# k and q as 32 by 32 squares: VectorE's block transpose in place of TensorE's turning, in an mLSTM cell with a SwiGLU block behind it

## The chip, the cores and the metric

The kernel runs on one core of one Trainium2 chip. The metric is the device time of a run in microseconds (us). The kernel before took 577.31 us (median of 3 runs, 577.21 to 579.02).

## What is computed

Two blocks follow each other. The first is an mLSTM cell over 4 batches of 8 heads, 768 tokens, head size 40, all float32. The second is a SwiGLU feed-forward block on its output, with model size 320 and inner size 1536. Cut to what matters:

```python
for t in range(S):
    m_new = np.maximum(f_gate[:, :, t] + m, i_gate[:, :, t])
    f_stab = np.exp(f_gate[:, :, t] + m - m_new)
    i_stab = np.exp(i_gate[:, :, t] - m_new)
    C = f_stab * C + i_stab * einsum('bhd,bhe->bhde', vt, kt)
    n = f_stab * n + i_stab * kt
    h_tilde = einsum('bhde,bhe->bhd', C, qt)
    denom = np.maximum(np.abs(einsum('bhd,bhd->bh', n, qt)), 1.0)
    y[:, :, t] = sigmoid(o_gate[:, :, t]) * h_tilde / denom
x = y.transpose(0, 2, 1, 3).reshape(B * S, H * D)
g = x @ w_gate
out = (g * sigmoid(g) * (x @ w_val)) @ w_out
```

The weights arrive as float64 and are narrowed to float32 in the kernel.

## The kernel before

The 768 tokens are cut into 6 groups of 128 (`NG`), each of two halves of 64. The cell works on a group at a time in the parallel form: scores of q against k, weights from the gates, a value product, and a running state C. The feed-forward block works on the same groups, 512 columns wide (4 batches of 128 tokens). While the feed-forward of group g runs, the cell of group n = g + 1 is computed between its pieces, and the inputs of group f = g + 2 are loaded. Nothing is scheduled by a planner: the order on every engine is the order in which the code issues (`manual_schedule`), and the pieces are put by hand into lists called `slots`, one list for each of 12 hidden chunks.

**The feed-forward.** `hidden` (L594) makes one chunk: 20 matmuls into two PSUM buffers of the tag "gen" (L599), of which there are four, then a silu on ScalarE (L604) and a product on VectorE (L605) that empty the two. Chunk m + 2 thus needs the buffers of chunk m. After 12 chunks, `project` (L612, matmuls L615) forms the output of each of the 4 batches; `result` (L607) copies it on ScalarE (L609, two buffers) and stores it from SyncE (L610). For group 0 `project_all` (L618, matmuls L622) does the four batches together, with a dictionary `after` (L689) of cell work between its 12 steps.

**Where k and q go.** `load` (L112) brings k and q with tokens on partitions: 128 partitions by 16 heads by 40 numbers, two such transfers to a tensor and group, issued on SyncE (L113). The scores (L305, matmuls L309) need them with the head dimension on partitions, in `kT` and `qT`: 128 partitions (two heads of 64, of which 40 are filled) by 16 head pairs by 128 tokens. `turn` (L299) makes these: for each half of the heads, `turn_one` (L289) runs 16 transposes for k and 16 for q on TensorE against an identity (L294, tile `tp_kq`), into PSUM buffers of the tag "cell", and copies them out, one copy on ScalarE and one on VectorE each (L117, L119). `add` (L325, matmuls L330), the state's increment, takes k as loaded, with tokens on partitions. `attend` (L344) reads qT again.

**The order around it.** Group 0 and group 1 have their own code; group 1's turning stands in slots 6 and 7 of the first hidden phase (L676, L677). For group 2, the loads of v, k, q and o_gate are issued during `project_all(0)` (L691, L693), behind the weights' load (`weights_load`, L400). After `project_all(0)` come the exponentials of the weights and the sigmoids of o_gate on ScalarE (L701 to L704) and the value products on GpSimd (`weigh_values`, L705, L706). Then the memory of the first phase is released and the pool `late` takes it (L707, L708). In the loop over g from 1 (L712), slots 0 and 1 hold `turn` for the two halves of the heads of group n (L716, L717), slot 3 the scores (L718), slot 5 the state's increment (L720), slots 7 and 9 `attend`; the loads of group f stand in slots 1 (q), 5 (k), 9 (v and weights) and 10 (o_gate) (L728 to L731).

Of the kernel before, what the change touches and what calls it, by code (L numbers as in the profile page):

```python
# [9 lines left out]
F32 = mybir.dt.float32  # L10
# [8 lines left out]
L = 128  # L19
# [5 lines left out]
def kernel(  # L25
# [18 lines left out]
    nc = tc.nc  # L44
    B, H, S, D = q.shape
# [4 lines left out]
    PP = BH // 2  # L50
# [8 lines left out]
    UA = UH // 2  # L59
# [16 lines left out]
    def bank(name, tag="cell"):  # L76
        return psum.tile([128, 512], F32, name=name, tag=tag)

    def half(i):
        return slice(i * SUB, (i + 1) * SUB)  # L80
# [4 lines left out]
    k_sb = const.tile([128, BH, DP], F32)  # L85
    q_sb = const.tile([128, BH, DP], F32)
    v_sb = const.tile([128, BH, D1], F32)
    o_sb = const.tile([128, BH, D], F32)
    w_sb = const.tile([128, BH, SUB], F32)
    vw_sb = const.tile([128, BH, D1], F32)  # L90
    kT = const.tile([128, PP, L], F32)
    qT = const.tile([128, PP, L], F32)
# [22 lines left out]
    def copy(eng, dst, src):  # L115
        if eng is nc.scalar:
            nc.scalar.copy(dst, src)  # L117
        else:
            eng.tensor_copy(dst, src)  # L119
# [125 lines left out]
    for u in range(B):  # L245
        r = slice(u * BH, (u + 1) * BH)
# [42 lines left out]
    def turn_one(P, src, dst, engs):  # L289
        tp = [bank("tp_kq").rearrange("p (a t) -> p a t", t=SUB) for _ in range(2)]  # L290
        for a in range(UA):
            h = P * UH + 2 * a
            for i in range(2):
                nc.tensor.transpose(tp[i][:, a, :], src[half(i), h:h + 2, :].rearrange("p h d -> p (h d)"),  # L294
                                    ident[half(i), half(i)])
        for i in range(2):
            copy(engs[i], dst[:, P * UA:(P + 1) * UA, half(i)], tp[i])

    def turn(P, eng_k, eng_q):  # L299
        turn_one(P, k_sb, kT, eng_k)  # L300
        turn_one(P, q_sb, qT, eng_q)

    QUAD = ((0, 0), (1, 1), (0, 1), (1, 0))

# [13 lines left out]
    def weigh_values(eng, P):  # L318
        eng.tensor_tensor(vw_sb[:, heads(P)], v_sb[:, heads(P)], w_sb[:, heads(P), last].to_broadcast([128, UH, D1]),  # L319
                          op=ALU.mult)  # L320
# [84 lines left out]
    def weights_sub(n, P):  # L405
        gb = g_T[:, n, heads(P)].unsqueeze(2).to_broadcast([128, UH, SUB])
        nc.vector.tensor_tensor(w_sb[:, heads(P)], gb, w_sb[:, heads(P)], op=ALU.subtract)  # L407

    def weights_mask(P):
        for i in range(2):  # L410
            w = w_sb[half(i), heads(P)]
            nc.gpsimd.affine_select(w, w, compare_op=ALU.is_ge, fill=NEG, base=0, pattern=[[0, UH], [1, SUB]],  # L412
                                    channel_multiplier=-1)

    def weights_exp(P):
        nc.scalar.activation(w_sb[:, heads(P)], w_sb[:, heads(P)], AF.Exp)

    def sig(P):
        nc.scalar.activation(o_sb[:, heads(P)], o_sb[:, heads(P)], AF.Sigmoid)
# [10 lines left out]
    A, V, G = nc.scalar, nc.vector, nc.gpsimd  # L430
# [163 lines left out]
    def hidden(g, m, first=()):  # L594
        ps = [bank("gv_ps", "gen") for _ in range(2)]
        x = xT(g)
        for kc in range(NKC):
            for i in range(2):
                nc.tensor.matmul(ps[i], lhsT=wgv_sb[half(i), m, PAIRS[kc][i], :], rhs=x[half(i), kc, :],  # L599
                                 start=(kc == 0), stop=(kc == NKC - 1))  # L600
        for f in first:
            f()
        sg = work.tile([128, TW], F32, name="sg")
        nc.scalar.activation(sg, ps[0], AF.Silu)  # L604
        nc.vector.tensor_tensor(hid(g, m), sg, ps[1], op=ALU.mult)  # L605
# [6 lines left out]
    def project(g, u):  # L612
        p = bank("o_ps", "gen")[:, 0:DM]
        for m in range(NFC):
            nc.tensor.matmul(p, lhsT=hid(g, m)[:, ts(u, L)], rhs=wo_sb[:, m, :], start=(m == 0), stop=(m == NFC - 1))  # L615
        result(g, u, p)
# [43 lines left out]
    def load_all(dst, a, n):  # L660
        for P in range(2):
            load(dst, a, n, P)

    run = lambda f, *a: (lambda: f(*a))
# [6 lines left out]
    slots = {  # L671
        0: [run(first_state, 1, A), run(load_all, k_sb, k, 1), run(load_all, q_sb, q, 1), run(late_maxima)],
        1: [run(decay_rows), run(piece_load, 6, h_sb[:, NH - NKC:])],
        2: [run(late_turns), run(weights_load, 1)],
        3: [run(decay), run(load_all, v_sb, v, 1)],
        6: [run(turn, 0, (A, A), (A, V)), run(piece_load, 7)],  # L676
        7: [run(turn, 1, (A, A), (A, V)), run(weights_sub, 1, 0), run(weights_sub, 1, 1), run(weights_mask, 0),  # L677
            run(weights_mask, 1)],
        8: [run(weights_exp, 0), run(weights_exp, 1), run(weigh_values, G, 0), run(weigh_values, G, 1),
# [5 lines left out]
    for m in range(NFC):  # L685
# [2 lines left out]
            f()  # L688
    after = {  # L689
        0: [run(do_attend, 1, 1), run(convert, 14), run(sig, 0), run(sig, 1), run(do_gate, 0)],  # L690
        1: [run(do_gather, 1, 1), run(weights_load, 2), run(load_all, v_sb, v, 2)],  # L691
        2: [run(do_divide, 0), run(convert, 15)],
        3: [run(do_divide, 1), run(load_all, k_sb, k, 2), run(load_all, q_sb, q, 2), run(load_all, o_sb, o_gate, 2)],  # L693
        4: [run(convert, 16), run(seam, 1, 0, (A, V, A, V))],
        5: [run(seam, 1, 1, (A, V, A, V))],
        6: [run(convert, 17)],
# [11 lines left out]
    late = ctx.enter_context(tc.tile_pool(name="late", bufs=1))  # L708
    xTs.append(late.tile([128, NKC, TW], F32, name="xT1"))


    for g in range(1, NG):  # L712
        n, f = g + 1, g + 2
        slots = {m: [] for m in range(NFC)}
        if n < NG:
            slots[0] = [run(turn, 0, (A, V), (A, V))]  # L716
            slots[1] = [run(turn, 1, (A, V), (A, V))]  # L717
            slots[3] = [run(do_scores), run(do_weigh, 0)]  # L718
            slots[4] = [run(do_weigh, 1)]
            slots[5] = [run(do_add), run(do_state, 2 * n, 0)]  # L720
            slots[6] = [run(do_state, 2 * n, 1)]
            slots[7] = [run(do_attend, n, 0), run(do_gather, n, 0)]
            slots[8] = [run(do_divide, 0)]
            slots[9] = [run(do_attend, n, 1), run(do_gather, n, 1)]
            slots[10] = [run(do_divide, 1), run(seam, n, 0, (A, V, A, V))]
            slots[11] = [run(seam, n, 1, (A, V, A, V))]
        if f < NG:
            slots[1].append(run(load_all, q_sb, q, f))  # L728
            slots[5].append(run(load_all, k_sb, k, f))
            slots[9] += [run(load_all, v_sb, v, f), run(weights_load, f)]  # L730
            slots[10].append(run(load_all, o_sb, o_gate, f))  # L731
        for m in range(NFC):
            hidden(g, m)
            for s in slots[m]:
                s()
        for u in range(B):
            if f < NG and u < 2:
                weights_sub(f, u)
                weights_mask(u)
            if f < NG and u == 2:  # L740
                weights_exp(0)
                weights_exp(1)
                sig(0)
                sig(1)
                weigh_values(nc.gpsimd, 0)
                weigh_values(nc.gpsimd, 1)
            project(g, u)
# [30 lines left out]
```

## Time and profile before

| What | Value |
|---|---|
| median of 3 runs | 577.31 us |
| profiled execution | 579.26 us, of which the span of the profile 577.5 us |
| TensorE matmul busy | 567.9 us (98% of the span) |
| VectorE busy | 211.7 us (37%) |
| ScalarE busy | 151.0 us (26%) |
| GpSimd busy | 102.4 us (18%) |
| SyncE's and ScalarE's transfer queue | 127284 packets, 32.92 MB, 33.0% of 16 engines' span |
| turning, `tp_kq` L294, matmuls | 160 for k and 160 for q, 222 ns each, overlapping |
| copies out of `tp_kq` | 584 to 592 ns on ScalarE, 680 to 684 ns on VectorE |
| a k or q load, two transfers of 320 KB | 6.4 us (k) and 4.0 us (q) from issue to landing, median |

How to read the profile: the span is one execution on the chip, in us. PE is TensorE's matmul, DVE VectorE, ACT ScalarE, POOL GpSimd, and SPq SyncE's queue; L294 is line 294 of the kernel. A group of instructions is given as line, engine, operation, output and input, shape and count. The chain of waits is the work that ended last, followed back from the last instruction: at each step to what released it, or to the instruction before it on its engine. In the chain in order of time, the columns are start, length, what, and how many instructions were merged. In the table of stretches, each line is a stretch of time with its length, then busy time and number of instructions of PE, PE's weight loads, DVE, ACT and POOL, then the granted TensorE clock, the mean busy share of the DMA engines (over 1 where packets overlap), and the rate in GB/s. The time of a transfer's row on SyncE is that of issuing it, not of the movement.

### The profile page before, as it was taken

To read this page: it belongs to the slowest core of one execution; us is meant where nothing else is said; L and a number is where in the kernel's file an instruction comes from. 1 tells how busy PE (TensorE), PEld (TensorE's weight loads), DVE (VectorE), ACT (ScalarE), POOL (GpSimd) and SP (SyncE) were. 2 spreads that over 40 slices of the span, in tenths; PEclk is the share of its full clock that TensorE was granted. 3 is DMA by queue.
4 is the path that set the end of the run, shared out by engine and by line. 5 is a ranking of instruction groups with operands and counts; after the bars stand their busy time and mean duration, and the time that the engine had idled before them with its cause. 6 is when DMAs were issued, how large, how long until landed. Compare 5 with 4: busy or idle time off the path is not lost.

```text
span 577.5 us, 12169 instructions
## 1 busy us (share of the span) xinstructions
PE 567.9 (98%) x5407; PEld 332.0 (57%) x5407; DVE 211.7 (37%) x378; ACT 151.0 (26%) x237; POOL 102.4 (18%) x101
## 2 busy tenths in 40 slices
PE   9998998999999999999999999999999999999997
PEld 4955454765655676455576555567555567544475
DVE  5776595860325600234620224630223630011100
ACT  3366554427210223201115210114311010011100
POOL 2132345463001141001132001232001110000000
PEclk9999998999999999999999999999999999999999
DMA  9999992494141800313620304450000000000000
GB/s 126 182 283 175 177 252 93 86 148 93 25 48 24 144 23 24 47 24 48 112 43 33 48 1 56 78 92 23 12 2 2 3 1 24 23 1 0 1 23 23
DMA packets 129915, 37.85 MB, mean 66 GB/s; under 512 B 120424, under 2 KB 125032, under 8 KB 129864
## 3 DMA queue, kind: packets, MB, share of 16 engines
q1 hardware_dynamic: 127284, 32.92, 33.0%
q10 hardware_dynamic: 2580, 4.16, 3.3%
q8 instruction: 42, 0.69, 0.5%
q14 instruction: 9, 0.07, 0.0%
HBM read 33.06 MB, written 4.01 MB: 64 GB/s over the span
## 4 chain that ended last, share of the span: by engine, by line
PE 91%; DMA 3%; ACT 3%; DVE 1%; issue 1%; POOL 0%; ACTq 0%; DVEq 0%; POOLq 0%
PE gv_ps L599 49%; PE o_ps L615 23%; PE o_ps L622 4%; DMA raw<-in_moe_w_val_dram 3%; PE inter L349 2%; PE intra L354 2%; PE add L330 2%; PE tp_kq L294 1%; PE sp L309 1%; PE first_y L486 1%; PE tp_x L395 1%; PE burn L425 1%; PE tp_x L517 1%; PE tp_kq L465 1%; PE sp L475 1%
## 5 line engine op out<-in xcount | busy, mean ns | idle before, releaser
L599 PE MATMUL gv_ps<-xT,wgv_sb 64*128 64x512 f32 x1440 | 322.2, 596 | 1.8 <-POOL wgv_sb L204 1.8
L599 PEld LDWEIGHTS gv_ps<-xT,wgv_sb 64*128 64x128 f32 x1440 | 139.6, 188 | 154.9 <-issue 150.2
L605 DVE TENSOR_TENSOR h_sb<-sg,gv_ps 128x512 f32<-128x512 f32 x72 | 49.5, 687 | 302.5 <-ACT sg L604 287.3
L615 PE MATMUL o_ps<-wo_sb,h_sb 128*128 128x320 f32 x480 | 130.5, 433 | 0.0
L615 PEld LDWEIGHTS o_ps<-wo_sb,h_sb 128*128 128x128 f32 x480 | 90.8, 190 | 38.2 <-issue 0.8
L604 ACT ACTIVATE sg<-gv_ps 128x512 f32<-128x512 f32 x72 | 43.0, 598 | 262.2 <-PE gv_ps L599 262.1
L339 POOL TENSOR_TENSOR C<-C,dec 128x328 f32<-128x328 f32 x20 | 14.5, 737 | 164.0 <-DVE C L341 164.0
L609 ACT COPY z_sb<-o_ps 128x320 f32<-128x320 f32 x24 | 10.2, 426 | 114.1 <-PE o_ps L615 102.7
L412 POOL TENSOR_SCALAR_AFFINE_SELECT w_sb<-w_sb 64x1024 f32<-64x1024 f32 x20 | 28.2, 1408 | 27.0 <-DVE w_sb L407 26.0
L622 PE MATMUL o_ps<-wo_sb,h_sb 128*128 128x320 f32 x96 | 26.9, 437 | 0.0
L375 POOL TENSOR_TENSOR o_sb<-o_sb,y_sb 128x640 f32<-128x640 f32 x10 | 14.2, 1428 | 48.6 <-DVE y_sb L366 48.6
L622 PEld LDWEIGHTS o_ps<-wo_sb,h_sb 128*128 128x128 f32 x96 | 17.9, 190 | 7.2
L366 DVE TENSOR_TENSOR y_sb<-y_sb,intra 64x328 f32<-64x328 f32 x40 | 19.7, 493 | 1.1
L319 POOL TENSOR_TENSOR vw_sb<-v_sb,w_sb 128x656 f32<-128x656 f32 x10 | 12.8, 1305 | 32.2 <-issue 32.2
L204 POOL TENSOR_TENSOR wgv_sb<-both,low 128x640 int32<-128x640 int32 x8 | 13.4, 1670 | 25.4 <-DVE both L197 25.4
L197 DVE SCALAR_TENSOR_TENSOR both<-top,both 128x640 uint32<-128x640 uint32 x18 | 15.7, 871 | 0.6
L349 PEld LDWEIGHTS inter<-C,qT 64*64 64x64 f32 x640 | 10.2, 134 | 7.3 <-issue 6.8
L196 DVE TENSOR_SCALAR both<-top 128x640 uint32<-128x640 uint32 x18 | 10.5, 581 | 9.3 <-ACT top L186 7.4
L330 PEld LDWEIGHTS add<-vw_sb,k_sb 64*64 64x64 f32 x640 | 10.5, 136 | 5.7 <-issue 4.9
L341 DVE TENSOR_TENSOR C<-C,add 128x328 f32<-128x328 f32 x20 | 9.9, 494 | 9.5 <-POOL C L339 9.3
L204 POOL TENSOR_TENSOR wo_sb<-both,low 128x640 int32<-128x640 int32 x6 | 10.2, 1700 | 17.4 <-DVE both L197 13.9
L407 DVE TENSOR_TENSOR w_sb<-g_T,w_sb 128x1024 f32<-128x1024 f32 x10 | 13.1, 1349 | 0.0
(120 smaller groups left out, 385.1 us busy)
## 6 DMA issues: line engine op xcount, KB each, us to landing
w_sb<-M_dram SPq DMA_DIRECT2D x10, 512.0 KB, 6.5
k_sb<-in_k_dram SPq DMA_DIRECT2D x12, 320.0 KB, 6.4
q_sb<-in_q_dram SPq DMA_DIRECT2D x12, 320.0 KB, 4.0
v_sb<-in_v_dram SPq DMA_DIRECT2D x12, 320.0 KB, 6.1
o_sb<-in_o_gate_dram SPq DMA_DIRECT2D x12, 320.0 KB, 6.8
raw<-in_moe_w_out_dram SPq DMA_DIRECT2D x3, 1280.0 KB, 7.2
out_dram<-z_sb SPq DMA_DIRECT2D x24, 160.0 KB, 1.8
h_sb<-in_moe_w_gate_dram SPq DMA_DIRECT2D x2, 640.0 KB, 9.0
```

The source lines that it names most:

```text
L197: nc.vector.scalar_tensor_tensor(both, in0=top, scalar=0x80000000, in1=both, op0=ALU.bitwise_and, op1=ALU.bitwise_or)
L204: (eng or nc.gpsimd).tensor_tensor(dst.bitcast(I32), both.bitcast(I32), lo, op=ALU.add)
L330: nc.tensor.matmul(ps[i][half(two), a, :], lhsT=k_sb[half(i), h, :], rhs=vw_sb[half(i), h, :], start=True, stop=True)
L339: nc.gpsimd.tensor_tensor(state(s + 1)[:, a], state(s)[:, a], dec[:, s - 2, a].unsqueeze(2).to_broadcast([128, UA, D1]), op=ALU.mult)
L349: nc.tensor.matmul(inter[two][half(i), a, :], lhsT=qT[half(two), P * UA + a, half(i)], rhs=state(2 * n + i)[half(two), P * UA + a, :], sta ...
L366: nc.vector.tensor_tensor(t, t, intra[i][half(c)], op=ALU.add)
L412: nc.gpsimd.affine_select(w, w, compare_op=ALU.is_ge, fill=NEG, base=0, pattern=[[0, UH], [1, SUB]], channel_multiplier=-1)
L599: nc.tensor.matmul(ps[i], lhsT=wgv_sb[half(i), m, PAIRS[kc][i], :], rhs=x[half(i), kc, :], start=(kc == 0), stop=(kc == NKC - 1))
L604: nc.scalar.activation(sg, ps[0], AF.Silu)
L605: nc.vector.tensor_tensor(hid(g, m), sg, ps[1], op=ALU.mult)
L615: nc.tensor.matmul(p, lhsT=hid(g, m)[:, ts(u, L)], rhs=wo_sb[:, m, :], start=(m == 0), stop=(m == NFC - 1))
L622: nc.tensor.matmul(ps[u], lhsT=hid(g, m)[:, ts(u, L)], rhs=wo_sb[:, m, :], start=(m == 0), stop=(m == NFC - 1))
```

## The change

From group 2 on, q is no longer loaded with tokens on partitions but as squares of 32 tokens by 32 numbers of the head dimension (the second square of a head holds the 8 that are left; the rest stays zero). A square's tokens lie on 32 partitions, chosen by head of the pair and by square: 16 transfers to a tensor and group, each of 32 partitions by 16 head pairs by 32 or 8 numbers. k is loaded twice: as before for the state's increment, and as squares into a new tile `k_sq` in the pool `late`. Two VectorE transposes to a tensor and group, each over 128 partitions by 1024 numbers, write kT and qT; `turn` is called for group 1 alone. For group 2 (g = 1) both stand in slot 2; for later groups q's in slot 0 and k's in slot 1. The loads of both squares for group f stand in slot 2. GpSimd zeroes the whole of q's tile during `project_all(0)` and `k_sq` behind the value products, ahead of its first load.

```diff
+    SQ = 32
+    def load_squares(dst, a, c):
+        for two in range(2):
+            for s in range(2):
+                r = slice((2 * two + s) * SQ, (2 * two + s + 1) * SQ)
+                w = min(SQ, D - s * SQ)
+                for t in range(L // SQ):
+                    nc.sync.dma_start(out=dst[r, :, t, 0:w],
+                                      in_=a[:, two:H:2, ds(c * L + t * SQ, SQ), ds(s * SQ, w)].rearrange("b h p d -> p (b h) d"))
+    def turn_squares(src, dst):
+        for P in range(2):
+            a = slice(P * UA, (P + 1) * UA)
+            nc.vector.transpose(out=dst[:, a].rearrange("p a t -> p (a t)"), in_=src[:, a].rearrange("p a t d -> p (a t d)"))
+    q_sq = q_sb.rearrange("p (a x) d -> p a (x d)", x=2).rearrange("p a (t d) -> p a t d", d=SQ)
...
-        1: [run(do_gather, 1, 1), run(weights_load, 2), run(load_all, v_sb, v, 2)],
+        1: [run(do_gather, 1, 1), run(weights_load, 2), run(load_all, v_sb, v, 2),
+            run(nc.gpsimd.memset, q_sb, 0.0)],
         2: [run(do_divide, 0), run(convert, 15)],
-        3: [run(do_divide, 1), run(load_all, k_sb, k, 2), run(load_all, q_sb, q, 2), run(load_all, o_sb, o_gate, 2)],
+        3: [run(do_divide, 1), run(load_all, k_sb, k, 2), run(load_squares, q_sq, q, 2), run(load_all, o_sb, o_gate, 2)],
...
+    k_sq = late.tile([128, PP, L // SQ, SQ], F32, name="k_sq")
+    nc.gpsimd.memset(k_sq, 0.0)
+    load_squares(k_sq, k, 2)
...
-            slots[0] = [run(turn, 0, (A, V), (A, V))]
-            slots[1] = [run(turn, 1, (A, V), (A, V))]
+            slots[2 if g == 1 else 0] = [run(turn_squares, q_sq, qT)]
+            slots[2 if g == 1 else 1] += [run(turn_squares, k_sq, kT)]
...
-            slots[1].append(run(load_all, q_sb, q, f))
+            slots[2] += [run(load_squares, q_sq, q, f), run(load_squares, k_sq, k, f)]
             slots[5].append(run(load_all, k_sb, k, f))
```

## The prediction

> **What bounds the kernel now.** I read the page's busy times and chain shares first, then the chain of waits in order of time, then SyncE's timeline and the table of stretches, each where the change cuts in.
>
> ```profile
> PE 567.9 (98%) x5407; PEld 332.0 (57%) x5407; DVE 211.7 (37%) x378; ACT 151.0 (26%) x237; POOL 102.4 (18%) x101
> PE 91%; DMA 3%; ACT 3%; DVE 1%; issue 1%; POOL 0%; ACTq 0%; DVEq 0%; POOLq 0%
> ```
>
> TensorE is busy for 98% of the span and 91% of the chain. VectorE, at 37%, has room. So PE time taken away shortens the run, unless a wait takes its place. The chain shows what the turning costs in a quiet group (start, length, what):
>
> ```profile
> 225.58 4.49 PE gv_ps L599 x20
> 230.07 0.99 PE tp_kq L294 x32
> 231.06 4.35 PE gv_ps L599 x20
> 235.41 0.99 PE tp_kq L294 x32
> 236.40 8.64 PE gv_ps L599 x40
> 245.03 2.02 PE sp L309 x128
> ...
> 496.15 51.70 PE gv_ps L599 x240
> ```
>
> Two visits of 0.99 us lie bare between hidden chunks of 20 matmuls; nothing hides them. The last line is the measure of an undisturbed chunk: 51.70 / 12 = 4.308 us. Groups g = 2, 3 and 4 look alike. Group g = 1, the first to meet the change, does not:
>
> ```profile
> 132.92 0.44 ACT z_sb L609
> 133.37 1.83 DMA out_dram<-z_sb
> ...
> 143.03 0.61 ACT sg L604
> 143.66 0.23 DVE h_sb L605
> ...
> 146.31 8.64 PE gv_ps L599 x40
> 154.95 2.02 PE sp L309 x128
> ```
>
> Here the chain leaves PE. ScalarE waits for an output transfer, then runs two exponentials, two sigmoids and three table loads before the first silu at 143.03. PE has only four PSUM buffers for hidden chunks, so chunk 2 cannot start before the product at 143.66 to 144.35 has emptied chunk 0's. SyncE just before that (start, length of issuing):
>
> ```profile
> 115.39 3.81 SPq L113 DMA_DIRECT2D k_sb<-in_k_dram  x2
> 119.25 6.17 SPq L113 DMA_DIRECT2D q_sb<-in_q_dram  x2
> 125.53 4.04 SPq L113 DMA_DIRECT2D o_sb<-in_o_gate_dram  x2
> 132.83 3.25 SPq L610 DMA_DIRECT2D out_dram<-z_sb  x4
> ```
>
> SyncE has 3.3 us between the last o_gate load and the first output transfer. And the rate of the transfers (last column GB/s):
>
> ```profile
> 110.00:112.00 2.00, 2.00 (x9) 1.38 (x8) 1.92 (x4) 0.38 (x1) 2.00 (x2) 1.00 1.19 256
> 118.00:120.00 2.00, 2.00 (x8) 1.14 (x6) 0.85 (x3) 0.39 (x2) 1.53 (x1) 1.00 1.51 161
> 120.00:122.00 2.00, 2.00 (x26) 1.61 (x26) 0.89 (x2) 1.25 (x3) 0.00 (x0) 1.00 1.56 136
> ```
>
> From 110 to 112 the weights move in pieces of 256 bytes (64 numbers), each transfer into 64 partitions: 256 / 256 = 1.0 piece per ns. From 118 to 122 k and q move in pieces of 160 bytes (40 numbers): 161 / 160 and 136 / 160, or 1.0 and 0.85 per ns. The rate counts pieces, not bytes, and half the partitions as target do not lower it.
>
> [...] with PE busy 0.76 of 2 us from 93 to 95 the clock is 0.57 from 95 to 97, and that chunk takes 5.90 us, not 4.35.
>
> **The change, part by part.**
>
> *PE, groups g = 2 to 4.* From 225.58 to 245.03 are 19.45 us. Without the visits it is 4.49 + 3 x 4.308 = 17.41. Gain 2.04 us a group, 6.1 us for three.
>
> *VectorE and ScalarE in those groups.* Four copies of 0.68 us leave VectorE and four of 0.59 us leave ScalarE. Four transposes of 128x1024 come in. The nearest row, the subtraction L407 of 128x1024, takes 1.21 us at the median[...]. I take 1.22 us[...]. Per slot 2.4 us stand behind the product of the chunk (0.69): 3.1 of 4.3 us. Queued behind them is the next product, which has 3.5 us of idle before it now (236.07). kT is read two chunks later. Cost nothing; at 2.4 us each still nothing, since the next two slots add no transposes and the lateness is worked off; only above about 3 us each would PE wait for the scores.
>
> *DMA in those groups.* A q or k load becomes 16 transfers of 32 x 16 = 512 pieces (128 bytes, or 32 for the tail), 8192 pieces in place of 4096, and k's squares come on top of k itself. They are issued in slot 2, some 50 us and more before use. Behind them on SyncE stands k_sb at slot 5 (257.0): 16384 pieces from 238 on end at about 255. Cost nothing.
>
> *Before g = 1: zeroing q and its squares.* GpSimd's memset: 128x768 took 0.73 us and 128x128 0.21, so 2048 takes 1.8. It falls near 112.4; x_sb's copy and L204 move by up to 1.8 us, with PE taking x_sb at 116.89 (3 us of cover) and wo_sb over 4 us later. Nothing. The 8192 pieces of q at 0.95 per ns take X = 8.6 us in place of about 4.4. SyncE is then free of o_gate at 129.57 + 4.2 = 133.8, the first output transfer starts 1 us late and behind pieces still draining: I take 1.5 us in sum (bounds 0 and 2.5). Every step of ScalarE up to the first silu moves with it.
>
> *g = 1.* GpSimd ends its vw_sb products at 140.8 + 1.5, zeroes k_sq (1.8) until 144.1, and only then SyncE may load k's squares: X = 8.6 and about 2 us to landing (1.83 for the output) make 154.7. PE: chunk 2 starts at 144.35 + 1.5 = 145.9 (now 146.09, the tp_kq visits gone), ends at 150.2; its product ends at 151.7; q's transposes run to 154.1; k's from 154.7 to 157.1. Chunk 3 is done at 154.5, the first half of the scores waits for kT until 155.9, and the second ends at about 158.1 where scores now end at 156.97. Loss 1.1 us. Behind the waiting transposes stands chunk 3's product, whose buffers chunk 5 needs: later than the scores. So the 3.6 us of turning and stall there are spent on the squares.
>
> In general, with d = X - 7.1 as ScalarE's delay, the scores end at 140.9 + 2X, a loss of 2X - 16.1: each us on a load counts twice. For X below 7.1 the delay is nil and q's transposes are late last: scores end at 156.0, a gain of 1.0.
>
> **Sum.** -6.1 + 1.1 = -5.0 us. The profiled execution took 579.26 us (span 577.5, 1.8 around it), 1.95 above the median of 577.31; I take the difference off the median: 572.3.
>
> **Rivals.**
> (a) *The squares are somewhat late.* X between 10.3 and 12 (0.8 to 0.68 pieces per ns, from overhead of 16 small transfers): loss 4.4 to 7.9 at g = 1 against 6.1 gained: 575.6 to 579.1, no change. For it: the rate falls to 0.85 at worst. Against: the pieces are smaller than any shown.
> (b) *The square loads are the bound: slower.* If a piece into a quarter of the partitions costs double (0.5 per ns), X = 16.4: loss 16.7 at g = 1, and PE idle that long starts at half clock (1.5): 577.31 - 6.1 + 18.2 = 589.4. It decides from X = 12 up. For it: no row shows 32 partitions, or 32 bytes. Against it: 64 partitions ran at 1.0, and in later groups even X = 16 is hidden.
> (c) *Transposes of 32-bit numbers at a quarter of the rate*, 4.4 us each: PE waits some 6 us for the scores in each of four groups, 577.31 - 8 + 24, about 593. Nothing speaks for it but the missing row.
> (d) *PE was not the bound, the gain doesn't come.* 98% busy speaks against it; under 1 in 50, within (a).
>
> **How the numbers follow.** The forecast with X up to 10.3 has 0.67, with its own range 569.8 to 575.6; (a) 0.13, (b) 0.16, (c) 0.04. About 0.3% (1.7 us) is what a measurement here tells from no change: faster 0.67, same 0.13, slower 0.20. For 8 in 10 I start at 569.8 (X small, gain 1.0, with 0.4 of scatter) and go to 580.5, the end of (a) with a half-clock window of 1.5.
>
> **What would show it.** Right: no tp_kq rows after 76 us; gv_ps unbroken over slots 0 to 2 at 4.3 us a chunk in g = 2 to 4; VectorE rows of 128x1024 near 1.2 us; at g = 1 the scores end near 158, with kT from VectorE as what PE waited for. Wrong: scores at g = 1 past 163, q's or k's squares taking over 10 us, ScalarE's first silu there past 146, or any wait of PE for kT in g = 2 to 4.

## The result and the profile after

| | before | after |
|---|---|---|
| median | 577.71 us (6 runs, 576.91 to 579.02) | 574.39 us (6 runs, 572.99 to 576.33) |
| profiled execution | 579.26 us, span 577.5 | 574.24 us, span 572.5 |

The ratio of the times is 0.9943, with a 95% interval of 0.9922 to 0.9964: 3.3 us faster, between 2.1 and 4.5. The forecast was 572.3 us, in a range of 569.8 to 580.5; the gain was forecast as 5.0 us, above the end of the measured interval.

The page's busy times and the engines' shares of the chain of waits, after:

```profile
PE 562.0 (98%) x5151; PEld 326.4 (57%) x5151; DVE 221.9 (39%) x378; ACT 142.9 (25%) x221; POOL 105.8 (18%) x103
PE 86%; DMA 5%; SPq 4%; ACT 3%; issue 1%; DVE 1%; POOL 0%; ACTq 0%; DVEq 0%; POOLq 0%
```

256 matmuls of turning are gone, VectorE's busy time is up by 10.2 us and ScalarE's down by 8.1. TensorE's busy time fell by 5.9 us and the span by 5.0: TensorE is still what the span is made of. Its smaller share of the chain (86% in place of 91%) is mostly at the start: there the chain now follows the first loads (SyncE's issuing up to 21.3 us, then a transfer of 12.48 us), which the change does not touch.

The chain in order of time, in the quiet group g = 2 and at its last line (start, length, what; all lines of the code have moved by 20, so the hidden chunks are L619 and the scores L329):

```profile
227.56 17.37 PE gv_ps L619 x80
244.92 2.02 PE sp L329 x128
...
491.57 51.70 PE gv_ps L619 x240
```

The four chunks of slots 0 to 3 have become one unbroken line of 80 matmuls. They took 19.45 us with the turning and take 17.37 without. The other two quiet groups show the same 17.37. The scores follow within 0.02 us, so nothing waits for kT.

The same chain at g = 1:

```profile
132.46 3.86 DMA out_dram<-z_sb
...
136.42 0.33 ACT z_sb L629
...
144.52 0.61 ACT sg L624
...
145.17 11.28 PE gv_ps L619 x40
...
156.49 2.20 PE sp L329 x128
```

Two things differ from before. The output transfer, for which ScalarE waits, took 3.86 us in place of 1.83. SyncE needed 1.43 of these to issue it, the first of four stores; before, issuing the first store took 0.36 (first line after, second before):

```profile
132.46 1.43 SPq L630 DMA_DIRECT2D out_dram<-z_sb  x1
132.83 0.36 SPq L610 DMA_DIRECT2D out_dram<-z_sb  x1
```

And chunks 2 and 3 took 11.28 us in place of 8.64. TensorE's own timeline (start, length, instruction; in brackets the idle time ahead of it and what ended it) and the table of stretches (PE, PE's loads, DVE, ACT, POOL, then granted clock, DMA share, GB/s) tell why:

```profile
133.52 8.85 PE L619 MATMUL gv_ps<-xT,wgv_sb 64*128 64x512 f32 x40
145.17 11.27 PE L619 MATMUL gv_ps<-xT,wgv_sb 64*128 64x512 f32 x40 [2.80 <-ACT sg L624]
156.49 2.20 PE L329 MATMUL sp<-qT,kT 64*64 64x64 f32 x128
```

```profile
144.00:146.00 2.00, 0.83 (x3) 0.41 (x5) 0.85 (x2) 1.59 (x3) 0.72 (x2) 1.00 0.35 52
146.00:148.00 2.00, 2.00 (x8) 1.40 (x9) 0.43 (x1) 0.00 (x0) 0.00 (x0) 0.67 0.75 90
148.00:150.00 2.00, 2.00 (x8) 1.51 (x6) 0.00 (x0) 0.00 (x0) 0.00 (x0) 0.50 0.64 58
```

TensorE idles for 2.80 us until ScalarE's late silu frees a PSUM buffer. After that the granted clock is 0.67 and then 0.50; microsecond by microsecond from 146 it is 0.84, three times 0.50 and 0.95, which makes 3.4 us at half clock. They cost 1.7: the same two chunks took 9.57 us in experiments 4 and 5, where the clock was 1.00. The scores have no bracket, so no wait for a transpose is recorded; but kT's second transpose ended only at 157.47, and the scores took 2.20 us where they had taken 2.02, so it was close.

**Where the time went**, by the two profiled executions. Group 1 begins 0.37 us earlier. From there to the start of group 2's hidden phase it loses 2.35 us: chunk 0 to the end of the scores is 158.69 - 133.52 = 25.17 in place of 156.97 - 133.89 = 23.08, a loss of 2.09, and 0.26 is lost later. The three quiet groups gain 6.56: from 225.58 to 496.15 are 270.57 us, from 227.56 to 491.57 are 264.01. The end is 0.42 shorter. Together -0.37 + 2.35 - 6.56 - 0.42 = -5.0. What the change itself did is -6.56 + 2.35 = -4.2 us, inside the interval of the medians. That the two profiled executions lie exactly the predicted 5.0 apart is luck: 0.8 of it lies ahead of group 1 and behind the quiet groups, where nothing of the turning stood.

### The profile page after: what moved, and what is told of

The parts are those of the page before. It is cut to its first block, busy times and chain, and to the rows that moved or that the text cites. A ratio compares the mean times of both kernels' runs of the same rounds, so it can differ in the third digit from the quotient of the medians.

```text
span 572.5 us, 11789 instructions
## 1 busy us (share of the span) xinstructions
PE 562.0 (98%) x5151; PEld 326.4 (57%) x5151; DVE 221.9 (39%) x378; ACT 142.9 (25%) x221; POOL 105.8 (18%) x103
## 4 chain that ended last, share of the span: by engine, by line
PE 86%; DMA 5%; SPq 4%; ACT 3%; issue 1%; DVE 1%; POOL 0%; ACTq 0%; DVEq 0%; POOLq 0%
PE gv_ps L619 50%; PE o_ps L635 23%; PE o_ps L642 4%; SPq L113 3%; DMA raw<-in_moe_w_val_dram 3%; DMA h_sb<-in_moe_w_gate_dram 2%; PE inter L369 2%; PE intra L374 2%; PE add L350 2%; PE sp L329 1%; PE tp_x L415 1%; DMA out_dram<-z_sb 1%; DVE w_sb L336 0%; ACT L624 0%; ACT L436 0%
## 5 line engine op out<-in xcount | busy, mean ns | idle before, releaser
L619 PE MATMUL gv_ps<-xT,wgv_sb 64*128 64x512 f32 x1440 | 323.3, 599 | 3.9 <-ACT sg L624 2.8
L619 PEld LDWEIGHTS gv_ps<-xT,wgv_sb 64*128 64x128 f32 x1440 | 142.6, 188 | 161.2 <-issue 151.5
L629 ACT COPY z_sb<-o_ps 128x320 f32<-128x320 f32 x24 | 10.2, 426 | 116.2 <-PE o_ps L635 102.7
L369 PEld LDWEIGHTS inter<-C,qT 64*64 64x64 f32 x640 | 10.2, 134 | 7.3 <-issue 6.8
L389 DVE TENSOR_SCALAR den<-den 128x16 f32<-128x16 f32 x10 | 14.0, 1402 | 0.3
L204 POOL TENSOR_TENSOR wo_sb<-both,low 128x640 int32<-128x640 int32 x6 | 10.2, 1700 | 15.7 <-DVE both L197 12.2
```

Source lines behind the costliest of these rows:

```text
L204: (eng or nc.gpsimd).tensor_tensor(dst.bitcast(I32), both.bitcast(I32), lo, op=ALU.add)
L369: nc.tensor.matmul(inter[two][half(i), a, :], lhsT=qT[half(two), P * UA + a, half(i)], rhs=state(2 * n + i)[half(two), P * UA + a, :], sta ...
```

## The experiments

The theory after the result: the turning in quiet groups is worth 6.2 us, free of any counter-cost, and group 1 gives part of it back, since q's longer load delays an output store, ScalarE's first silu, and with it TensorE. The rivals: the squares of k are what is late there; or the transposes, the extra loads and the memsets cost something wherever they are. Each ratio below is taken against runs of the kernel before that were made beside it; their medians went from 577.71 to 578.60, so medians of different experiments compare no better than that.

**1. Squares from group 3 on, group 2 as before.**

```diff
-            run(nc.gpsimd.memset, q_sb, 0.0)],
...
-        3: [..., run(load_squares, q_sq, q, 2), ...],
+        3: [..., run(load_all, q_sb, q, 2), ...],
...
-    load_squares(k_sq, k, 2)
...
+            if g == 1:
+                slots[0] = [run(turn, 0, (A, V), (A, V))]
+                slots[1] = [run(turn, 1, (A, V), (A, V))]
+                slots[2] = [run(nc.gpsimd.memset, q_sb, 0.0)]
```

> Group 2 is loaded and turned as before the change; squares only from group 3 on. Theory (the gain is 2.08 us in each of three quiet groups, the loss of about 2.1 us at g = 1 comes from group 2's squares alone): the loss goes, 577.7 - 6.2 = 571.5, gv_ps and tp_kq at g = 1 as before, scores there end near 157. Rival (the loss comes from the longer zeroing, the third tile or the transposes' order, or the gain is smaller than the chain shows): 573.5 to 575, as with the change.

Measured: 572.9 us (571.13 to 577.28), ratio 0.9896 (0.9854 to 0.9939). Its chain at g = 1:

```profile
144.88 8.64 PE gv_ps L619 x40
153.52 2.02 PE sp L329 x128
```

Chunks 2 and 3 are back at 8.64 us. From chunk 0 at 132.46 to the scores' end at 155.54 are 23.08 us, exactly the number of before, and the quiet groups keep their gain. So the loss of 2.09 us comes from group 2's squares, and in this execution the half clock is gone with it (granted clock 1.00 throughout). The median lies 1.5 below that of the change, with overlapping intervals; the chain, not the median, carries this.

**2. q's squares of group 2 behind the output stores**, so that the stores go first.

```diff
-        3: [..., run(load_squares, q_sq, q, 2), run(load_all, o_sb, o_gate, 2)],
+        3: [..., run(load_all, o_sb, o_gate, 2)],
     project_all(0, after)
+    load_squares(q_sq, q, 2)
```

> As the change, but q's squares of group 2 are issued behind the four output stores of group 0. Theory (two causes one behind the other: the delayed store holds ScalarE and with it chunk 2, and k's squares land just in time behind it): ScalarE's first silu is back near 142.7, chunk 2 starts near 144, but k's squares now follow q's and land near 155, so the scores still end near 158.6 and nothing is won: 574 to 576. Rival (the delayed store and the half clock behind it are the whole loss): the scores end near 156.5 and the time is 572 to 572.7.

Measured: 575.34 us (573.38 to 578.28), ratio 0.9936 (0.9909 to 0.9963): no better than the change. TensorE's timeline:

```profile
141.62 9.57 PE L619 MATMUL gv_ps<-xT,wgv_sb 64*128 64x512 f32 x40 [0.92 <-ACT sg L624]
154.84 3.69 PE L329 MATMUL sp<-qT,kT 64*64 64x64 f32 x128 [3.65 <-DVE kT L319]
```

The store is quick again and the wait for the silu falls from 2.80 to 0.92, without half clock. But the scores now wait 3.65 us for kT, since k's squares stand behind q's on SyncE and land just ahead of 153.45, and half clock comes with that idle time (granted clock 0.97 from 152 to 154 us, then 0.50 to 160; the scores take 3.69 us, not 2.02). One late thing was removed and the next one showed.

**3. k of group 2 turned on TensorE at g = 1**, and its squares not loaded; q's squares stay where the change has them.

```diff
-    load_squares(k_sq, k, 2)
...
+            if g == 1:
+                slots[0] = [run(turn_one, 0, k_sb, kT, (A, V))]
+                slots[1] = [run(turn_one, 1, k_sb, kT, (A, V))]
+                slots[2] = [run(turn_squares, q_sq, qT)]
```

> As the change, but k of group 2 is turned on TensorE in slots 0 and 1 of g = 1 from its tokens, so no squares of k are needed for it; q's squares stay ahead of o_gate. Theory: k's squares no longer bound the scores, but the delayed store still holds ScalarE by about 1.6 us, chunk 2 starts near 145.1 as with the change; TensorE's idle time there is 1 us shorter: 571.5 to 573, the lower end if the half clock does not come. Rival (k's squares were not late, the store is all): 574.

Measured: 573.13 us (572.1 to 575.43), ratio 0.9892 (0.9853 to 0.993).

```profile
144.65 12.30 PE L619 MATMUL gv_ps<-xT,wgv_sb 64*128 64x512 f32 x40 [2.76 <-ACT sg L624]
```

The wait for the silu is there in full (2.76, not 1 us shorter as I had expected), with half clock from 144 to 151 around it (granted clock 0.52, 0.50, 0.50 and 0.77 in the stretches of 2 us from 144 on): taking k's squares away does not touch the first wait.

**4. Both: stores first, and k on TensorE at g = 1.** The edits of 2 and 3 together:

```diff
-        3: [..., run(load_squares, q_sq, q, 2), run(load_all, o_sb, o_gate, 2)],
+        3: [..., run(load_all, o_sb, o_gate, 2)],
     project_all(0, after)
+    load_squares(q_sq, q, 2)
...
-    load_squares(k_sq, k, 2)
...
+                slots[0] = [run(turn_one, 0, k_sb, kT, (A, V))]
+                slots[1] = [run(turn_one, 1, k_sb, kT, (A, V))]
+                slots[2] = [run(turn_squares, q_sq, qT)]
```

> Both at once: k of group 2 turned on TensorE, q's squares of group 2 behind the output stores. Theory: both causes are gone, ScalarE's silu is at its old place, chunk 2 starts near 144 and the scores end near 155: 577.7 - 6.2 - 1.7 = 569.8, the best of all. Rival (something else at g = 1 costs 2 us): 571.5 or more.

Measured: **569.64 us** (568.54 to 572.58), ratio 0.9839 (0.9801 to 0.9878). Its interval lies wholly below that of the change: this version beats both kernels. TensorE's timeline:

```profile
141.50 9.57 PE L619 MATMUL gv_ps<-xT,wgv_sb 64*128 64x512 f32 x40
151.00 2.09 PE L329 MATMUL sp<-qT,kT 64*64 64x64 f32 x128
```

No bracket, so no long wait. The two chunks take 9.57 us at a granted clock of 1.00, not 8.64: chunk 2 starts when the silu has emptied one of its two PSUM buffers (140.84 to 141.44), and then waits for the product to empty the other (141.48 to 142.17). From chunk 0 to the scores' end are 153.09 - 131.72 = 21.37 us, 1.71 less than before and 3.80 less than after. Of the two repairs, alone one gave nothing (575.34 against 574.39) and the other 1.3 us, with overlapping intervals; together they gave 4.8. The two late arrivals lay beside each other, and either was enough to hold TensorE in the profiles.

**5. Filling TensorE's idle time.** Three matmuls on data that nobody uses are added to the change behind chunk 1 of g = 1.

```diff
+    def fill(n):
+        t = bank("burn")
+        for _ in range(n):
+            nc.tensor.matmul(t, lhsT=ident, rhs=wo_sb.rearrange("p m d -> p (m d)")[:, 0:512], start=True, stop=True)
...
+            if g == 1:
+                slots[1] = [run(fill, 3)]
```

> The change as it is, with three float32 matmuls of 128x512 on data nobody reads, put on TensorE behind chunk 1 of g = 1, where it stood idle for 2.8 us (work is added). Theory (idle time drops the clock and that costs about 1 us net, after which k's squares are the next wait): no half clock there, chunks 2 and 3 take about 9.3 us in place of 11.3, the scores wait for kT and end near 157.7 in place of 158.7: 573.4. Rival (the half clock is hidden by k's squares or not caused by idling): 574.4, chunks 2 and 3 at 11.3 us.

Measured: 574.62 us (572.24 to 576.72), ratio 0.993 (0.9909 to 0.995): not to be told from the change. The timeline (lines from here on moved by 5; the three matmuls show as six rows):

```profile
145.12 2.84 PE L450 MATMUL burn<-wo_sb,ident 128*128 128x512 f32 x6
148.03 9.57 PE L624 MATMUL gv_ps<-xT,wgv_sb 64*128 64x512 f32 x40
158.57 2.29 PE L329 MATMUL sp<-qT,kT 64*64 64x64 f32 x128 [0.97 <-DVE kT L319]
```

In this execution the idle time is filled, the clock there stays at 1.00 and chunks 2 and 3 take 9.57 in place of 11.27. That agrees with the idle time as the cause of the half clock; one execution doesn't show it, since half clock comes and goes here with the same idle time too (last section). And now the scores wait 0.97 us for kT: behind the silu, k's squares were nearly as late. Chunk 0 to the scores' end is 160.86 - 136.34 = 24.52, only 0.65 below the change and 1.44 above before: what the place costs at full clock. The expectation of a faster median failed.

**6. The same filling with k on TensorE**, to price the half clock by itself.

```diff
+            if g == 1:
+                slots[1].append(run(fill, 3))
```

> k of group 2 is turned on TensorE (as in the kernel that did this alone, 573.13 us), q's squares stay ahead of o_gate, and three matmuls of 128x512 on data that nobody uses are added behind chunk 1 of g = 1, where TensorE idled for 2.76 us. They add work of 2.84 us and change nothing of the output. No transpose waits for a load there any more, so this prices the half clock by itself. Both theories expect no half clock from 140 to 152 and chunks 2 and 3 in 9.57 us as in the kernel with full clock there (12.30 without the filling). Theory A (the half clock comes in most executions): the time falls by about 2.4, to some 570.7. Theory B (it came in the profiled executions by chance and is rare in the others): the time stays at 573.

Measured: 576.88 us (573.15 to 582.13, 22 runs), ratio 0.996 (0.9942 to 0.9979). Both theories missed. The timeline:

```profile
146.01 2.84 PE L450 MATMUL burn<-wo_sb,ident 128*128 128x512 f32 x6 [2.21 <-ACT kT L117]
148.78 8.86 PE L624 MATMUL gv_ps<-xT,wgv_sb 64*128 64x512 f32 x40
```

The filling did not fill. It takes a PSUM buffer that turning also uses, so it waited 2.21 us for ScalarE's copy of kT, which stands behind the late silu, and then lay on the path with its 2.84 us. The clock did stay at 1.00 there. Chunk 2 starts 2.23 us later after chunk 0 than in experiment 3 (14.88 against 12.65), and the two chunks are 3.44 shorter, so from chunk 0 to the scores' end this profile is 1.2 us shorter (25.76 against 26.98). Yet the median is 3.7 us longer, and the intervals don't meet. That speaks for theory B, that the half clock at g = 1 is rare in experiment 3's other executions; it doesn't show it, since the mean granted clock of these runs is lower too (0.9915 against 0.9945), by about one half-clock stretch that the profiles don't place.

**7. Both ways at once**: groups 3 to 5 are turned on TensorE and also loaded as squares and transposed, into a tile that nobody reads.

```diff
...
+                slots[0] = [run(turn, 0, (A, V), (A, V)), run(turn_squares, q_sq, spare)]
+                slots[1] = [run(turn, 1, (A, V), (A, V)), run(turn_squares, k_sq, spare)]
...
+            slots[1].append(run(load_all, q_sb, q, f))
```

> Groups 3 to 5 do both: TensorE turns k and q from their tokens as before the change, and the squares of both are loaded and transposed too, into a tile that nobody reads (work is added, the output doesn't change). Group 2 as before. Theory (square loads and transposes are hidden in the quiet groups, and the gain is TensorE's turning alone): the time of the kernel before, 577.7, within 1 us. Rival (the loads or transposes cost something there that the gain covered): 579.5 or more.

Measured: 577.66 us (576.27 to 581.33), ratio 0.9986 (0.9962 to 1.0011). Its chain in the quiet group:

```profile
227.47 4.49 PE gv_ps L619 x20
231.97 0.99 PE tp_kq L294 x32
...
246.93 2.02 PE sp L329 x128
```

246.93 - 227.47 = 19.46 us against 19.45 before. In quiet groups the square loads and the transposes cost nothing; the gain is TensorE's 2.08 us and nothing else.

**8 and 9. The transposes two and three times**, on the kernel of experiment 1.

```diff
-                slots[0] = [run(turn_squares, q_sq, qT)]
-                slots[1] = [run(turn_squares, k_sq, kT)]
+                slots[0] = [run(turn_squares, q_sq, qT)] * 2
+                slots[1] = [run(turn_squares, k_sq, kT)] * 2
```

> The kernel with squares from group 3 on, each VectorE transpose done twice (4.8 us in each of slots 0 and 1). Theory: below the 3 us per transpose at which TensorE comes to wait, so nothing: 572.9, within 1 us. Rival (VectorE is near its limit there): each of three groups loses 2 us or more, 579 or more.

> The same, each transpose done three times (7.2 us in each of slots 0 and 1, 15.8 us of VectorE from chunk 0 to kT with the products). Theory: the product of chunk 1 is late by 0.7 us for chunk 3, and kT by some 3 us for the scores: 3 to 4 us in each of three groups, 572.9 + 9 to 12 = 582 to 585, and up to 1.7 more a group if the half clock comes. Rival (the waits run side by side and two slots of room absorb them): under 575.

Measured: 573.84 us (572.17 to 575.29) for two, 577.2 us (575.73 to 580.66) for three. The chain for two and TensorE's and VectorE's timeline for three:

```profile
226.22 17.37 PE gv_ps L619 x80
243.59 2.02 PE sp L329 x128
```

```profile
227.17 17.88 PE L619 MATMUL gv_ps<-xT,wgv_sb 64*128 64x512 f32 x80
246.24 2.20 PE L329 MATMUL sp<-qT,kT 64*64 64x64 f32 x128 [1.19 <-DVE kT L319]
```

```profile
233.00 6.87 DVE L319 STREAM_TRANSPOSE qT<-q_sb 128x1024 f32<-128x1024 f32 x6
```

Doubled, the transposes are still hidden: 17.37 us, no wait. Tripled, they show, as a wait of 1.19 us for kT and 0.5 in the chunks. From chunk 0 to the scores' end by the chain: 248.44 - 227.24 = 21.20 us a group against 245.61 - 226.22 = 19.39, 1.8 each. I had expected 3 to 4. The end of the cover, between two and three times, was right, its slope not: three times costs a total of 4.3 by the medians.

**10. No turning at all** from group 2 on, on the kernel before; the scores then use group 1's qT and kT.

```diff
-            slots[0] = [run(turn, 0, (A, V), (A, V))]
-            slots[1] = [run(turn, 1, (A, V), (A, V))]
```

> The kernel before without any turning from group 2 on: the two calls of turn in slots 0 and 1 are left out, q and k are loaded as before, no squares and no transposes; qT and kT keep group 1's values, so the scores, and with them the output, are of other data. This is the most that taking the turning off TensorE can give. Theory (the transposes, the square loads and the memsets cost nothing where they are hidden; only the crossing of loads and waits at g = 1 costs): the same as the best version so far, which turns k on TensorE at g = 1 alone and loads q's squares behind the stores: 569.6, within 1. Rival (VectorE's transposes or the extra pieces take something everywhere): 567 or less. In the quiet groups chunks 0 to 3 take 17.37 us in both.

Measured: 570.39 us (569.13 to 572.71), ratio 0.9858 (0.9826 to 0.9891). The chain:

```profile
141.61 9.57 PE gv_ps L599 x40
...
221.96 17.37 PE gv_ps L599 x80
```

The version of experiment 4, which does all the work, is as fast as the kernel that leaves the turning out (0.9839 and 0.9858, overlapping intervals; 17.37 us in both). So there is nothing measurable left to be had from the turning.

## Why the prediction was right, and where it was off

The direction, the range and most of the working held; the gain by the medians, 3.3 us, is smaller than the 5.0 forecast. By the profiled executions the change itself is worth 4.2, and the difference to 5.0 lies at g = 1. What makes the medians smaller still is not shown.

**The quiet groups: right.** Forecast 2.04 us each, measured 2.08, 6.24 in sum and 6.56 with what lies around.

**The transposes: right.** 1.22 us was put, my estimate from the subtraction's 1.21 us, since no row of before shows a transpose; 1.20 to 1.24 were measured. Here VectorE's timeline at g = 1:

```profile
152.85 2.36 DVE L319 STREAM_TRANSPOSE qT<-q_sb 128x1024 f32<-128x1024 f32 x2
155.14 2.33 DVE L319 STREAM_TRANSPOSE kT<-k_sq 128x1024 f32<-128x1024 f32 x2
```

"At 2.4 us each still nothing" is confirmed by doubling them. "Above about 3 us each PE would wait" agrees with the wait at three times (6.87 us for what had been two transposes, 3.4 each).

**The square loads: right for k, too small for q.** X was put at 8.6 us. k's squares at g = 1 took 8.30 on SyncE, the squares for groups 3 to 5 took 8.3 to 10.3 and stayed hidden. q's squares for group 2 took 11.73, so one of my signs of being wrong, squares of over 10 us, did come. Behind the output stores the same load took 8.66 (experiment 2), so the rest goes with its place behind v's and k's loads. This moved the issue of o_gate from 8.36 to 3.04 us ahead of chunk 0, 5.3 us later where I had 4.2. But o_gate's own issue then took 1.83 us in place of 4.04:

```profile
118.66 11.73 SPq L313 DMA_DIRECT2D q_sb<-in_q_dram  x16
130.48 1.83 SPq L113 DMA_DIRECT2D o_sb<-in_o_gate_dram  x2
132.46 5.22 SPq L630 DMA_DIRECT2D out_dram<-z_sb  x4
144.05 8.30 SPq L313 DMA_DIRECT2D k_sq<-in_k_dram  x16
```

So SyncE was free at 132.3, not at 133.8, and began to issue the first output store on time. The delay comes after that, in the issuing (1.43 us in place of 0.36) and in the landing, 3.86 us after the start of the issue in place of 1.9 (before, ScalarE's next copy starts at 134.75, and the issue had started at 132.83). The sum for ScalarE, 1.5 us, is what the clock times show (first silu at 144.52 in place of 143.03); against the start of chunk 0 it is 1.86.

**The loss at g = 1: the mis-sized term.** Forecast 1.1 us, measured 2.09. "Chunk 2 starts at 145.9 and ends at 150.2" priced the chunk at full clock, as if the idle time ahead of it were free. By the forecast's own numbers TensorE would stand idle for some 3.3 us there, by my estimate (133.89 and two chunks of 4.35 us make 142.6). It idled 2.80 us, the granted clock fell to 0.50, and two chunks took 11.28 us, not 8.64. Of the 2.64 us more, 1.7 are the half clock; most of the rest is chunk 2's wait for the product, which I had put ahead of its start. So chunk 3 ended 2.3 us later than forecast, counted from chunk 0, and the wait of 1.4 us for kT that I had put behind it did not come: two errors that partly cancel. I had named the half clock, with 1.5 us, only in rival (b) and at the end of the range, for much longer waits. The profile of before spoke against that: its stretch from 93 to 95 us, behind which the clock was 0.57, has only two short gaps, of 1.41 and 0.32 us.

**"kT from VectorE as what PE waited for": wrong.** In the profile no such wait is recorded: the half clock kept TensorE back until k's squares had nearly all been turned, and 0.2 us at most is left of the wait (the scores took 2.20 us, not 2.02). With the idle time filled, kT is what the scores wait for, 0.97 us (experiment 5), and the loss is 1.44; so at full clock the forecast wait is there, and 1.1 was near. That "each us on a load counts twice" was not tested as such; experiments 2 to 4 show that the two loads do not add, since removing one wait leaves the other.

**The rivals.** (a) put X at 10.3 to 12. q's 11.73 lies there, but the loss was 2.09 us, not 4.4 to 7.9: o_gate's issue became 2.2 us shorter, and k's squares took 8.30. (b) needed 16.4 and (c) 4.4 us for a transpose, and neither came; (d) falls with TensorE's 5.9 us.

**Open.** How often executions that were not profiled had the half clock at g = 1 is not settled. The mean granted clock of each run goes in steps of about 0.003, which is one stretch of 3.4 us at half clock like the one at g = 1 (1.7 of 572.5 us). The runs of the change read 0.991 or 0.994, so three stretches or two, by estimate. The profiled one has three, near 27, 95 and 147 us, and the first two are in the profile of before as well. In other kernels here the times moved with the mean clock too: in experiment 5 from 572.24 us at 1.000 to 576.72 at 0.988, in experiment 10 from 569.13 at 1.000 to 572.71 at 0.991. Experiment 5 removed the half clock at g = 1 in its profile, and its median did not move; experiment 6 failed to price it.

## What to carry to other kernels

Here removing work from the bounding engine paid in full (2.08 us a group) where the replacement was issued long before its use; look at the first group that meets the change, where the lead is shortest, since here the gain was right to 0.1 us a group and the error lay all at that place. When a transfer grows, look at what stands behind it in the same queue (here a small output store, then ScalarE's chain with three table loads of 1.28 us, then the matmuls), and price any new idle time of TensorE as a range, with the half clock that may follow it (here 1.7 us behind 2.80 us of idle time). When one repair at such a place brings nothing, try the second late arrival together with it before dropping either: 0 and 1.3 us alone were 4.8 together.

## What the runs showed of the hardware

**Half clock after 2.8 us of idle time, but not each time.** 2.80 us of idle time (after) and 2.76 (experiment 3) had half clock beside them (granted clock 0.50), 2.21 (experiment 6) did not (1.00). Near 93 us, ahead of the change, every kernel here has the same gap of 1.41 or 1.42 us. Half clock followed it in seven of the twelve profiles, before and after among them, and not in the other five (experiments 1 to 4 and 10). TensorE's timeline and the stretch from 96 to 98 us (granted clock 0.50 and 1.00), first after, then in experiment 1:

```profile
93.33 0.28 PE L350 MATMUL add<-vw_sb,k_sb 64*64 64x41 f32 x2 [1.41 <-DVE w_sb L336]
96.00:98.00 2.00, 2.00 (x6) 0.69 (x4) 0.96 (x3) 0.00 (x0) 1.14 (x2) 0.50 0.84 285
```

```profile
94.12 0.28 PE L350 MATMUL add<-vw_sb,k_sb 64*64 64x41 f32 x2 [1.41 <-DVE w_sb L336]
96.00:98.00 2.00, 2.00 (x10) 0.86 (x10) 0.99 (x2) 0.00 (x0) 1.39 (x3) 1.00 0.80 198
```

So a gap of 1.41 us was followed by half clock in some executions and not in others. And near 27 us half clock came with no gap in the profile: in before and after TensorE is busy in every stretch from 20 to 27 us, at a clock of 1.00, and from 27 to 28 us the clock is 0.50 and 0.61. What sets it is not shown.

**VectorE beside a GpSimd memset.** GpSimd's and VectorE's timeline, after, near the memset of q's tile:

```profile
108.98 2.83 POOL L395 TENSOR_TENSOR o_sb<-o_sb,y_sb 128x640 f32<-128x640 f32 x2
111.73 1.82 POOL L684 MEMSET q_sb<- 128x2048 f32 x1
```

```profile
110.49 3.09 DVE L389 TENSOR_SCALAR den<-den 128x16 f32<-128x16 f32 x1
```

An operation on 16 numbers a partition takes 3.09 us and ends at 113.58, when the memset does (113.55). Before, without the memset, it took 1.34 and ended at 112.36, with GpSimd's product at 112.33. In both profiles it thus ended within 0.03 us of GpSimd's instruction; what ties the two is not shown. It cost TensorE nothing there: the 32 matmuls beside it took 8.81 us in the chain, before and after.

**A small store behind many small pieces** landed 3.86 us after SyncE began to issue it, in place of 1.9, though the issue began on time; SyncE's own part grew from 0.36 to 1.43 us.

**Transposes back to back** take 6.87 us for six, 1.14 each, against 2.36 for two (experiment 9 and after).
